# The last two blocks' down projection: two levels of seven products over both blocks at once, in place of one level for each block

## The chip, the cores and the metric

The kernel runs on one core of one Trainium2 chip. The metric is the device time of one execution in microseconds. Before the change it is 1012.9 us, the median of three runs (1011.5 to 1014.69).

A core has five engines, each with its own instruction queue, which it works through in order: TensorE (PE; its weight loads are listed as PEld), VectorE (DVE), ScalarE (ACT), GpSimd (POOL) and SyncE (SP, which issues most of the DMAs). They meet through semaphores. TensorE writes to PSUM, in banks; the others evict from there to SBUF.

## The reference

Linear attention without softmax, a root-mean-square normalisation per head, and then a feed-forward block with a gate (SwiGLU), all in fp32:

```python
def _attn_ref(q, k, v, g_norm):          # q, k, v: (8, 8, 576, 64)
    kv = np.einsum('bhsd,bhse->bhde', k, v)
    out = np.einsum('bhsd,bhde->bhse', q, kv)
    rms = np.sqrt(np.mean(out * out, axis=-1, keepdims=True) + 1e-06)
    return (out / rms * g_norm).astype(np.float32)

def _moe_ref(x, w_gate, w_val, w_out):   # x: (4608, 512), d_ff = 1536
    g = x @ w_gate
    silu = g * (1.0 / (1.0 + np.exp(-g)))
    val = x @ w_val
    return (silu * val @ w_out).astype(np.float32)
```

## The kernel before

**Tiling.** The 4608 tokens are cut into nine blocks of 512. Blocks 0 to 2 go alone, then blocks (3, 4), (5, 6) and (7, 8) go as pairs. Each block or pair has an up phase (x by w_gate and w_val, then h = silu(g) * v) and a down phase (h by w_out); the attention of later blocks is placed into the gaps. All large products use Winograd's form of Strassen's scheme: a 2x2 block product with seven products in place of eight, with sums of the operands before and sums of the results after. The seven are numbered 1 to 7. `CHAIN` tells which PSUM tile each adds into: 1, 6, 7, 4 build up in one "b" bank one after another, 2 in "a", 5 and 3 in "c". Between two products of a chain the running value is read out, so TensorE may not start product 6 before product 1's value has been evicted, and so on.

**The up phase of a pair** (`Pair.up`, `Inner`, matmuls at L816) uses two levels, 7 x 7 = 49 products for each pair j of 128-wide columns of h, and there are six j. The outer products are taken in four groups g of up to two; in each group the seven inner products follow, one 128x256 matmul for each outer product. `Inner.sequence` weaves the last two products of a group into the next group. The 49 weights of a j were written to DRAM earlier and are read back through 14 DMAs (`Stream`, L906) into a pool of nine tiles `t`; `Stream.pump`, called after each product, issues the next load when the tile nine places back has been given up. All of them go through SP's queue.

VectorE evicts each product, adding it onto an earlier group's result. Four times in a j, GpSimd adds group 1's finished quarter (U2) to the result of outer product 5 (P5) into a third room, from where VectorE's evictions of group 3 read it (`made1`). Then GpSimd makes one more sum (`made2`), the two products silu(g) * v for both blocks (`made3`, 128x1024 each), and block a's two sums of h (`h_sums`). For the last j VectorE does the last two. Results live in a ring of five rooms `r`.

**The down phase** (`Ffn.down`, `Down`, matmuls at L661) uses one level, for block a and then for block b: seven products, each six steps times two halves, 84 matmuls of 128x256 for a block. Their stationary operand is h and their moving operand w_out; the result is in row order. The sums on w_out for products 5, 7 and 4 are made by GpSimd into tiles of the same pool (`turn_t`). For the last two blocks `down.lone` is set: nothing is left to weave in, so product 3 goes into an own bank "m" (`third`, L1032) and is placed earlier, and the last block (`final`) keeps its halves in banks apart, so that the last output half can be stored early (`store`, L1122).

**What sets the order.** Each engine's order is fixed when the program is built: by the order in which the code records instructions, by `tc.issue_after` (an instruction may not stand ahead of a given one), and by `in_order`, which pins an engine to the recorded order. Before, the pair's down phases pin TensorE.

The small sums and products all record through helpers, so their lines are L130 (add), L131 (subtract) and L132 (multiply) wherever they are used.

Of the kernel before, what the change touches and what calls it, by code (L numbers as in the profile page):

```python
# [14 lines left out]
P = 128  # L15
# [3 lines left out]
def kernel(  # L19
# [114 lines left out]
    @contextmanager  # L134
    def in_order(*engines):

        traced = nc.cur_bb.bb.instructions
        last = traced[-1]
        yield
        start = next(k for k in reversed(range(len(traced))) if traced[k] is last) + 1  # L140
        before = {}
        for i in traced[start:]:
            if engines and i.engine not in engines:
                continue
            if i.engine in before:
                tc.add_manual_dep(
                    i, before[i.engine].name,
                    mybir.DependencyInfo(mybir.DependencyClass.NoSync, mybir.DependencyReason.DATA), reason="order",
                )
            before[i.engine] = i  # L150

# [488 lines left out]
    class Quad:  # L640


        def __init__(self, steps):
            self.steps = steps
            self.ps, self.room = {}, None

            self.apart = {}

# [3 lines left out]
        def multiply(self, p):  # L652
            name, first = CHAIN[p]
            if first:
                tiles = [PSUMS[name].tile([P, 2, HB], F32, name=name) for _ in range(1 + (name in self.apart))]
                self.ps[name], self.apart[name] = tiles[0], tiles[-1]
            banks = self.ps[name], self.apart[name]
            for e, i in self.order(p):
                lhsT, rhs = self.operands(p, e, i)

                self.ffn.multiplied = nc.tensor.matmul(  # L661
                    banks[e][:, e], lhsT=lhsT, rhs=rhs, start=first and i == 0 and (e == 0 or banks[0] is not banks[1]),
                    stop=i == self.steps - 1, skip_group_check=True,
                )
            getattr(self, f"after{p}", lambda: None)()
# [91 lines left out]
    class Inner:  # L757
# [94 lines left out]
        def made3(self, p, e, q):  # L852
            if p != 4:
                return
            h = h_both[:, :, 2 * self.j : 2 * self.j + 2]
            halves = lambda t: t.rearrange("p (b e) t -> p b e t", b=2)
            c11, c12, c21, c22 = (self.whole(*i) for i in ((1, 1), (3, 1), (3, 0), (1, 0)))

            engine = nc.gpsimd if self.j + 1 < NP else nc.vector
            mul(engine, h[:, :, :, 0:HB], halves(c11), halves(c12))  # L860
            with tc.issue_after(self.ffn.fifth.ins):
                nc.scalar.activation(out=c21, in_=c21, func=ACT.Silu)
            mul(engine, h[:, :, :, HB:BLK], halves(c21), halves(c22))
            self.ffn.ended = self.ffn.a.h_sums(self.j, 1, engine)

# [13 lines left out]
    class Stream:  # L879
# [15 lines left out]
        def pump(self):  # L895

            while self.next and not self.held[-9]:
                n, j, c = key = self.next.pop(0)
                tile_ = t_tile(key)
                os, ps = JOINT[c]  # L900
                count = len(os) * len(ps)
                self.tiles[key] = tile_.rearrange("p a (b c) -> p (a b) c", c=P)
                self.uses[key] = count
                to = self.tiles[key][:, 0:count].rearrange("p (o i) c -> p o (i c)", o=len(os))
                src = self.dram[:, j, steps_of(OUTERS, os), steps_of(INNERS, ps)].rearrange("p o i c -> p o (i c)")
                nc.sync.dma_start(out=to, in_=src)  # L906

        def use(self, n, j, o, p):
            c, i = self.joint[o, p]
            key = n, j, c  # L910
            self.uses[key] -= 1
            if not self.uses[key]:
                self.free(key)
            return self.tiles[key][:, i]
# [4 lines left out]
    stream = Stream()  # L919
# [65 lines left out]
    class Down(Quad):  # L985
        def __init__(self, ffn):
            super().__init__(NP)
            self.ffn = ffn
            self.t = {}
            self.final = ffn.n == NB - 1  # L990
            self.lone = False
            self.opens = None
            self.keeps = False
            if self.final:
                self.apart["c"] = None
# [16 lines left out]
        def multiply(self, p, es=(0, 1)):  # L1012
            if p == 3 and self.lone:
                self.third(es)
                return
# [7 lines left out]
        def third(self, es):  # L1023


            if es[0] == 0:
                tiles = [m_psum.tile([P, 2, HB], F32, name="m") for _ in range(1 + self.final)]
                self.thirds = tiles[0], tiles[-1]
            for e in es:
                for i in range(self.steps):  # L1030
                    lhsT, rhs = self.operands(3, e, i)
                    self.ffn.multiplied = nc.tensor.matmul(  # L1032
                        self.thirds[e][:, e], lhsT=lhsT, rhs=rhs, start=i == 0 and (e == 0 or self.final),
                        stop=i == self.steps - 1, skip_group_check=True,
                    )
            if not self.final:
                add(nc.vector, self.o1[:, :, HD:DM], self.thirds[0], self.u2)
                self.ffn.store(self.o1, 0)
                return
            for e in es:  # L1040
                add(nc.vector, self.o1[:, e, HD:DM], self.thirds[e][:, e], self.u2[:, e])
                self.ffn.store(self.o1[:, e : e + 1, HD:DM], e, slice(HD, DM))

        def after6(self):
            super().after6()
            if self.lone:
                self.add_c(self.u2, self.u2)

        def order(self, p):
            order = [(e, i) for e in range(2) for i in range(self.steps)]  # L1050
            return order if p == 3 and self.final else sorted(order, key=lambda ei: ei[1])
# [17 lines left out]
        def rows(self):  # L1069
            o = ring()  # L1070
            self.o1, self.o2 = o[:, 0:2], o[:, 2:4]

        def after2(self):
            if self.lone:
                self.rows()
            add(nc.vector, self.o1[:, :, 0:HD], self.ps["a"], self.s)
            if self.final:
                self.ffn.store(self.o1[:, :, 0:HD], 0, slice(0, HD))
# [4 lines left out]
        def after7(self):  # L1083
            if not self.lone:
                self.rows()
            u3 = self.piece(2)
            nc.scalar.copy(out=u3, in_=self.ps["b"])
            self.add_c(self.o2[:, :, HD:DM], u3)
# [5 lines left out]
        def after3(self):  # L1094
            self.add_c(self.o1[:, :, HD:DM], self.u2)
            if not self.final:
                self.ffn.store(self.o1, 0)
                return
            for e in range(2):
                self.ffn.store(self.o1[:, e : e + 1, HD:DM], e, slice(HD, DM))  # L1100

        def add_c(self, o, u):

            if not self.final:
                add(nc.vector, o, self.ps["c"], u)
                return
            for e, c in enumerate((self.ps["c"], self.apart["c"])):
                add(nc.vector, o[:, e], c[:, e], u[:, e])

    class Ffn:  # L1110
# [9 lines left out]
        def store(self, o, t, columns=slice(None)):  # L1120
            rows = out[BLK * self.n : BLK * (self.n + 1), columns].rearrange("(t p) d -> p t d", t=T)
# [40 lines left out]
        def down(self, nxt, then={}):  # L1162
# [3 lines left out]
            down.lone = nxt is None  # L1166
            order = (1, 6, 5, 7, 2, 4, 3) if 5 in fill else (1, 5, 6, 7, 2, 4, 3)
            if down.lone:
                order = (1, 5, 6, 2, 7, 3, 4)
            for p in order:  # L1170
# [5 lines left out]
                with tc.issue_after(nxt.multiplied.ins) if self.n == 0 and p in (5, 6) else ExitStack():  # L1176
                    down.multiply(p, *[(0,)] * (p == 3 and down.lone and down.final))
# [14 lines left out]
            if down.lone and down.final:  # L1192
                down.multiply(3, (1,))
# [25 lines left out]
    class Pair:  # L1219


        def __init__(self, n):
            self.n = n
            self.a, self.b = (Ffn(i, blocks[i]) for i in (n, n + 1))
            self.visited = None

        def up(self, fill):

            a = self.a
            a.s1 = s_pool.tile([P, NP, HB], F32, name="s1")  # L1230
# [5 lines left out]
            for i, this in enumerate(units):  # L1236
                for unit, p in this.sequence(last):
                    if unit:
                        visited, self.visited = self.visited, None
                        with tc.issue_after(visited.ins) if visited else ExitStack():  # L1240
                            unit.multiply(p)
                last = this
                fill.get(i + 1, lambda: None)()
            a.down_ = Down(a)
            a.down_.keeps = True
            a.down_.turn_t(5)
# [3 lines left out]
            a.ended = self.ended  # L1250
# [165 lines left out]
    for n in range(PAIRED, NB, 2):  # L1416
# [3 lines left out]
        if after:  # L1420
# [10 lines left out]
            for i in range(8):  # L1431
                fill[12 + i] = lambda i=i, after=after: after[i // 4].load_quarters(i % 4 // 2, (i % 2,))
        pair.up(fill)
        if after:
            after[0].turn()
        if len(after) > 2:
            after[2].load_kv(0)
        with in_order(nc.tensor.engine):
            pair.a.down(after[0] if after else None, {5: pair.second_sums})
            if after:  # L1440
                after[1].turn()
            if len(after) > 2:
                after[2].load_kv(1)
            pair.b.down(after[1] if after else None)
# [31 lines left out]
```

## Time and profile before

| | us |
|---|---|
| median of the runs | 1012.9 |
| the profiled execution | 1012.7 |
| its span, first to last instruction | 1010.9 |
| TensorE busy | 993.7 |
| VectorE busy | 673.7 |
| GpSimd busy | 369.6 |
| ScalarE busy | 232.2 |

The granted TensorE clock is full in this execution. A fp32 matmul of the large products is recorded as two passes, so 84 matmuls show as 168. "Busy" of TensorE is not TensorE at its peak, since matmuls are pipelined. Times in timelines are microseconds from the start of the span. In a group's row the last part is the idle time of the engine just before these instructions, and which instruction ended it.

### The profile page before, as it was taken

The numbers are of one execution on the slowest core, as the hardware profiler recorded it, in microseconds if no ns is written. First come the engines' busy times: TensorE is split into PE (matmuls) and PEld (weight loads), VectorE is DVE, ScalarE is ACT, GpSimd is POOL, SyncE is SP. The second block draws the span as 40 slices with busy tenths as digits, with TensorE's granted clock in tenths as the row PEclk, the third lists the DMA queues.
The fourth block names the chain that finished last, engine by engine and source line by source line (L and its number), as shares of the span: only waits on it lengthen the run. The fifth ranks groups of instructions, "written<-read, shape, count | busy, mean of one in ns | idle before, by whom it ended". The sixth has DMA issues, their size and how long they took to land.

```text
span 1010.9 us, 17078 instructions
## 1 busy us (share of the span) xinstructions
PE 993.7 (98%) x6506; PEld 831.6 (82%) x6506; DVE 673.7 (67%) x1121; ACT 232.2 (23%) x367; POOL 369.6 (37%) x290
## 2 busy tenths in 40 slices
PE   5999999999999999999999999999999999999998
PEld 4544688888888888888888888888888888888887
DVE  2999797589868477656676746666668566666311
ACT  2665111221122311212211121121112121121000
POOL 0000263255544240445456004455660026546600
PEclk9999999999999999999999999999999999999999
DMA  8688653483866855767742464667221654553011
GB/s 220 198 266 260 120 93 136 97 288 97 210 136 122 214 114 158 189 179 182 170 130 42 111 164 135 182 164 191 77 42 43 146 164 144 150 145 101 1 42 42
DMA packets 254290, 143.23 MB, mean 142 GB/s; under 512 B 149504, under 2 KB 236544, under 8 KB 254208
## 3 DMA queue, kind: packets, MB, share of 16 engines
q1 hardware_dynamic: 223488, 138.20, 50.8%
q10 hardware_dynamic: 30656, 3.94, 2.5%
q8 instruction: 52, 0.85, 0.4%
q14 instruction: 30, 0.25, 0.1%
q0 software_dynamic: 64, 0.00, 0.0%
HBM read 104.99 MB, written 28.70 MB: 132 GB/s over the span
## 4 chain that ended last, share of the span: by engine, by line
PE 75%; DMA 1%; POOL 0%; SPq 0%; issue 0%; DVE 0%; POOLq 0%
PE b L816 22%; PE b L661 20%; PE c L816 11%; PE c L661 9%; PE a L816 5%; PE a L661 5%; PE m L431 1%; PE m L1032 1%; PE m L370 1%; DMA ld<-in_v_dram 1%; POOL t L131 0%; SPq L312 0%; PE b L370 0%; PE b L431 0%; PE a L431 0%
## 5 line engine op out<-in xcount | busy, mean ns | idle before, releaser
L816 PE MATMUL b<-arena,t 128*128 128x256 f32 x1008 | 244.5, 381 | 0.0
L816 PEld LDWEIGHTS b<-arena,t 128*128 128x128 f32 x1008 | 190.1, 190 | 29.6 <-DVE r L130 2.4
L130 POOL TENSOR_TENSOR r<-r 128x256 f32<-128x256 f32 (+1 forms) x90 | 94.7, 1054 | 246.1 <-DVE r L130 154.9
L130 DVE TENSOR_TENSOR r<-b,r 128x512 f32<-128x512 f32 (+1 forms) x234 | 138.9, 606 | 60.1 <-PE b L816 54.8
L130 DVE TENSOR_TENSOR r<-c,r 128x512 f32<-128x512 f32 (+1 forms) x170 | 104.5, 623 | 81.9 <-PE c L816 40.1
L132 POOL TENSOR_TENSOR arena<-r 128x1024 f32<-128x1024 f32 (+1 forms) x54 | 102.1, 1904 | 112.3 <-DVE r L130 67.9
L131 POOL TENSOR_TENSOR t<-wo 128x512 f32<-128x512 f32 x54 | 76.9, 1445 | 167.8 <-DVE wo L130 105.9
L130 DVE TENSOR_TENSOR r<-a,r 128x512 f32<-128x512 f32 x93 | 59.2, 636 | 108.3 <-PE a L661 70.7
L816 PE MATMUL c<-arena,t 128*128 128x256 f32 x504 | 122.5, 379 | 0.0
L131 DVE TENSOR_TENSOR arena<-arena 128x512 f32<-128x512 f32 (+3 forms) x96 | 104.3, 1101 | 20.0 <-PE b L661 17.7
L816 PEld LDWEIGHTS c<-arena,t 128*128 128x128 f32 x504 | 95.6, 190 | 13.5 <-issue 0.3
L661 PE MATMUL b<-wo,arena 128*128 128x256 f32 x432 | 98.1, 382 | 0.2
L661 PE MATMUL b<-t,arena 128*128 128x256 f32 x432 | 96.2, 379 | 0.0
L661 PEld LDWEIGHTS b<-wo,arena 128*128 128x128 f32 x432 | 81.2, 190 | 12.5 <-DVE arena L132 0.9
L661 PEld LDWEIGHTS b<-t,arena 128*128 128x128 f32 x432 | 82.1, 190 | 11.2
L830 ACT COPY r<-b 128x512 f32<-128x512 f32 x54 | 31.7, 586 | 189.9 <-PE b L816 189.9
L131 POOL TENSOR_TENSOR t<-arena 128x512 f32<-128x512 f32 x36 | 51.1, 1432 | 56.2 <-PE c L661 21.9
L816 PE MATMUL a<-arena,t 128*128 128x256 f32 x252 | 66.1, 379 | 0.0
L816 PEld LDWEIGHTS a<-arena,t 128*128 128x128 f32 x252 | 47.9, 190 | 6.5
L661 PE MATMUL c<-t,s 128*128 128x256 f32 x216 | 48.1, 379 | 0.0
L661 PE MATMUL a<-wo,arena 128*128 128x256 f32 x216 | 48.1, 379 | 0.0
L661 PEld LDWEIGHTS a<-wo,arena 128*128 128x128 f32 x216 | 41.0, 190 | 5.6
(115 smaller groups left out, 1242.9 us busy)
## 6 DMA issues: line engine op xcount, KB each, us to landing
t<-w SPq DMA_DIRECT2D x180, 256.0 KB, 3.1
out_dram<-r SPq DMA_DIRECT2D x17, 512.0 KB, 2.9
ld<-in_k_dram SPq DMA_DIRECT2D x26, 288.0 KB, 4.6
ld<-in_v_dram SPq DMA_DIRECT2D x26, 288.0 KB, 6.1
t<-w SPq DMA_DIRECT2D x54, 128.0 KB, 2.3
ld<-in_moe_w_gate_dram SPq DMA_DIRECT2D x12, 512.0 KB, 4.6
ld<-in_moe_w_val_dram SPq DMA_DIRECT2D x12, 512.0 KB, 4.7
ld<-in_moe_w_out_dram SPq DMA_DIRECT2D x12, 512.0 KB, 4.8
```

The lines of the kernel that those rows point to most:

```text
L130: add = lambda e, o, a, b: e.tensor_tensor(out=o, in0=a, in1=b, op=OP.add)
L131: sub = lambda e, o, a, b: e.tensor_tensor(out=o, in0=a, in1=b, op=OP.subtract)
L132: mul = lambda e, o, a, b: e.tensor_tensor(out=o, in0=a, in1=b, op=OP.mult)
L370: self.positions = nc.tensor.matmul(self.kv_ps[r][u * D : (u + 1) * D, g, :], lhsT=k[:, u, c, :], rhs=v[:, u, c, :], start=(c == 0), stop= ...
L431: self.multiplied = nc.tensor.matmul(self.ps[i][u][p : p + D, t, j, :], lhsT=self.qt[rows, tile_t, head, p : p + D], rhs=kvs[b % 3][rows, ...
L661: self.ffn.multiplied = nc.tensor.matmul(banks[e][:, e], lhsT=lhsT, rhs=rhs, start=first and i == 0 and (e == 0 or banks[0] is not banks[1 ...
L816: self.ffn.multiplied = nc.tensor.matmul(ps[:, i], lhsT=stream.use(self.ffn.n, self.j, o, p), rhs=self.operand(o, p), start=first and i == ...
L830: copied = nc.scalar.copy(out=dst, in_=ps)
L1032: self.ffn.multiplied = nc.tensor.matmul(self.thirds[e][:, e], lhsT=lhsT, rhs=rhs, start=i == 0 and (e == 0 or self.final), stop=i == self ...
```

## The change

The last pair (blocks 7 and 8) gets its own down phase, `Deep.down`, with both blocks together and two levels: 7 outer times 7 inner products, each of three steps c over d_ff, so 147 matmuls of 128x256. Now w_out is the stationary operand and h of both blocks the moving one, so the result is transposed: it is turned back at the end, two quadrants by VectorE's transposes of 32x32 pieces with the rest done in 32 small stores (`send`, half on ACT's queue, half on SP's), two by 16 TensorE transposes (`turn_back`).

The sums on w_out move to GpSimd in the pair's up phase (`Deep.prepare`, given out by `tick` after each product at the places in `TURNS`, every place in the first fourteen): six sums in place on w_out; nine blocks of differences for outer products 5, 7 and 4, each written to DRAM from the one buffer `temp` and read back later as 21 leaf tiles; and twelve differences for outer products 1, 2, 6 and 3, kept in SBUF. GpSimd also makes the h sums for both blocks, at least twelve places after h (`made`), and the inner sums of h for two of the three steps (`turn`). The remaining sums of h (`sum_x`, `outer`) are VectorE's, between the products of the down phase, whose order is written out by hand and pinned for TensorE and VectorE. The `lone` and `final` branches of the old down phase are removed; no other block used them.

```diff
+        def turned_block(self, i, c):
+            temp, rows = self.temp[:, 0:7], slice(2 * c, 2 * c + 2)
+            raw = temp[:, 0:4].rearrange("p (k n) d -> p k (n d)", k=2)
+            b, t2o = (self.quadrant(o)[:, rows] for o in ((3, 1, 2)[i], 6))
+            def differences():
+                sub(nc.gpsimd, temp[:, 4], temp[:, 0], temp[:, 1])
+                sub(nc.gpsimd, temp[:, 5:7], temp[:, 2:4], temp[:, 1:2].to_broadcast([P, 2, P]))
+                nc.sync.dma_start(out=self.dram[:, i, c], in_=temp)
+            return [lambda: sub(nc.gpsimd, raw, b, t2o), differences]
...
+            for i in range(3):
+                for c in range(3):
+                    self.later += self.turned_block(i, c) + [kept.pop(0)]
+            self.later += kept
+
+        TURNS = {0: (0, 1), 1: (), 2: (4, 5, 6), 3: (0, 2, 4, 5)}
+
+        def tick(self):
+            g, e = divmod(self.count % 28, 7)
+            self.count += 1
+            if e not in self.TURNS[g] and self.count > 14:
+                return
+            steps = self.due if self.due and self.due[0][0] <= self.count else self.later
+            step = steps.pop(0) if steps else None
+            if step:
+                with behind(nc.gpsimd.engine):
+                    (step[1] if steps is self.due else step)()
...
+        def sum_x(self, x, *os):
+            for o in os:
+                a11, a12, s2, a22 = (self.part(o, k, q) for k, q in ((0, 0), (1, 0), (0, 1), (1, 1)))
+                to = self.extras[o][:, x]
+                if x == 0:
+                    add(nc.vector, to, s2, a11)
...
+        def down(self):
...
+            m(2, 7)
...
+            add(nc.vector, v, u2, c22)
+            self.sum_x(0, 3)
+            m(2, 3)
+            self.sum_x(1, 3)
+            m(3, 1)
+            self.sum_x(2, 3)
+            room = ring().rearrange("p (o a) x -> p o (a x)", o=2)
+            add(nc.vector, c11, p1, c11)
+            m(2, 4)
+            nc.vector.transpose(out=room[:, 0], in_=c11)
+            self.send(room[:, 0], 0, 0, nc.scalar)
+            m(3, 6)
+            add(nc.vector, c22, u3, c22)
+            m(3, 5)
+            nc.vector.transpose(out=room[:, 1], in_=c22)
+            self.send(room[:, 1], 1, 1, nc.sync)
+            m(3, 2)
+            m(3, 7)
+            self.rows = ring().rearrange("p (e q) (o f d) -> p e q o f d", e=2, o=2, f=2)
+            m(3, 3)
+            self.turn_back(0, 0)
+            self.turn_back(1, 1)
+            m(3, 4)
+            self.turn_back(1, 0)
+            self.turn_back(0, 1, True)
...
+        if pair.deep:
+            stream.leaves(pair.deep)
+            pair.up(fill)
+            with in_order(nc.tensor.engine, nc.vector.engine):
+                pair.deep.down()
+            continue
```

## The prediction

> **What bounds the kernel now.** I read the page's busy times and slices, the chain that ended last, the groups with shapes kept apart, then the timelines of GpSimd and VectorE in the last pair, and the DMA issues.
>
> ```profile
> PE 993.7 (98%) x6506; PEld 831.6 (82%) x6506; DVE 673.7 (67%) x1121; ACT 232.2 (23%) x367; POOL 369.6 (37%) x290
> POOL 0000263255544240445456004455660026546600
> ```
>
> TensorE has work for 98% of the span; GpSimd has none in the last two slices and about half of each slice ahead of them. By stretch (busy us of TensorE, its weight loads, VectorE, ScalarE, GpSimd), the last pair's up and down phases:
>
> ```profile
> 807.80:935.00 127.20, 127.20 (x589) 111.45 (x588) 84.95 (x144) 25.71 (x35) 65.79 (x53) 1.00 0.47 140
> 935.00:1008.00 73.00, 72.54 (x337) 63.52 (x335) 16.77 (x20) 5.75 (x9) 16.29 (x12) 1.00 0.08 28
> ```
>
> GpSimd has 61 us to spare in the first, VectorE 56 us in the second.
>
> ```profile
> 910.22 0.86 PE a L816 x4
> ...
> 933.97 1.05 PE b L816 x4
> 935.02 5.18 PE b L661 x24
> ...
> 1004.95 2.60 PE m L1032 x12
> 1007.55 0.02 issue
> 1007.58 0.42 DVE r L130
> ```
>
> The chain is TensorE without a gap: the up phase of 127.2 us, then the two down phases to 1007.5. A 128x256 product is recorded as two passes; 24 passes take 5.18 us, so a pass takes 0.216 and a product 0.432 us. Fewer products are worth that much each, if nothing else comes late.
>
> ```profile
> L132 POOL TENSOR_TENSOR arena<-r 128x1024 f32<-128x1024 f32 x30 | 70.2, 2361 | 60.7 <-DVE r L130 60.7
> L130 POOL TENSOR_TENSOR r<-r 128x256 f32<-128x256 f32 x72 | 52.3, 728 | 187.8 <-DVE r L130 96.6 <-DMA t<-w 89.1
> L132 DVE TENSOR_TENSOR arena<-r 128x1024 f32<-128x1024 f32 x6 | 7.1, 1222 | 0.3
> 818.28 1.53 POOL L130 TENSOR_TENSOR r<-r 128x256 f32<-128x256 f32 x2 [59.84 <-DVE r L130]
> 820.81 0.72 POOL L130 TENSOR_TENSOR r<-r 128x256 f32<-128x256 f32 x1 [1.00 <-DVE r L130]
> 832.59 4.68 POOL L132 TENSOR_TENSOR arena<-r 128x1024 f32<-128x1024 f32 x2 [3.79 <-DVE r L130]
> 923.46 1.28 POOL L131 TENSOR_TENSOR t<-wo 128x512 f32<-128x512 f32 x1
> 844.27 0.69 DVE L130 TENSOR_TENSOR r<-b,r 128x512 f32<-128x512 f32 x1 [0.36 <-PE b L816]
> t<-w SPq DMA_DIRECT2D x180, 256.0 KB, 3.1
> w<-arena SPq DMA_DIRECT2D x10, 384.0 KB, 3.5
> out_dram<-r SPq DMA_DIRECT2D x17, 512.0 KB, 2.9
> ```
>
> In the up phase GpSimd's U2 + P5 pieces (818.28 to 822.9) are read by VectorE's evictions of group 3, so GpSimd can hold up VectorE, and VectorE holds a bank that TensorE wants.
>
> [...] the up phase's evictions read one from PSUM, and GpSimd's 128x1024 products stay at 2.34 each there, so I take uncontended durations. [...] the rows above show 2.9 to 3.5 us for writes of 384 and 512 KB.
>
> **The change: TensorE.** Removed: 2 x 84 = 168 products of L661 and L1032. Added: 49 x 3 = 147 of the same shape, and 16 transposes of 128x128 (L494: 16 in 2.3 us, 0.14 each). 21 x 0.432 = 9.1 us saved; 8 transposes stand ahead of the last product (1.2 us).
>
> **The change: VectorE in the down phase.** It had 16.8 us to do there. Now: 33 sums of 128x768, not in the trace; 0.69 us at 512 and 1.22 at 1024 bound them, and I take 0.95: 31.4 us. Evictions: 13 x 0.69 + 11 x 0.42 = 13.6. Five operations at 1024, 1.22 each: 6.1. Two transposes at 1.22: 2.4. Six sums of 512 at 0.70: 4.2. Two copies: 0.8. Together 58.5 us, under TensorE's 147 x 0.432 + 16 x 0.14 = 65.8, but in a fixed order. Walking that order from the start of down: VectorE is 3 us ahead at the first extras, level with TensorE when the sums for outer product 5 are made (18 to 27 us), and about 3 us behind around 45 us, where V, the sums for 4 and 3 and the first eviction of group 3 are queued. There inner product 6 of group 3 waits for that eviction about 1.5 us (none with sums at 0.87, 2.5 with 1.0). Then TensorE leads again. **The end:** last product at 66.4, its eviction 0.2 + 0.7, four transposes 0.6 + 0.2, two copies 0.8: VectorE ends at 68.8 us, where before it took 73.0 from the start of down (935.0 to 1008.0). The 32 small stores of 32 KB go out from 53 us (ACT) and 57 us (SP). Issues of 64 KB pieces took 0.63 us, so sixteen take 10 us and leave SP free at about 67.5, just in time for the last four tiles; up to 1 us more if slower. The store after it is 128 KB as before. **Down gives 4.2 us (2.5 to 5.5).**
>
> **The change: GpSimd in the last up phase.** Kept: 24 pieces at 0.73, six sums and ten products at 2.36: 55.3 us. Added: six sums on w_out at 1.28 (7.7); nine leaf blocks, each 512 + 128 + 256 wide, 1.28 + 0.45 + 0.73 (22; the 0.45 is the line through 256 and 512); twelve 384-wide differences at 1.0 (12); ten h sums at 1.28 (12.8, replacing 7.3); eight turned sums at 1.28 (10.2). 120 us of 127 where it had 65.8: it fits over the whole phase, but most comes first, in the engine's fixed order. There is one buffer for a leaf block: each block's first subtraction waits until the last block's 448 KB write to DRAM has landed. That write is not in the trace; 2.9 to 3.5 us bound it, I take 3.2.
>
> Walk down GpSimd's queue as the changed program orders it, from the up phase's start (0 = 807.8); "wanted" is when VectorE or TensorE came to that point before (its evictions at 823.1, 824.0, 825.3 and 844.27). The w_out sums may start as the last product of the block before frees w_out, at -4, and end at 4.5 (with 0.08 between dependent operations). Block 1 ends at 7.1, its write lands at 10.4. A 1.0 us difference covers part of that. Block 2 starts at 10.5 and ends at 13.1, landing at 16.4. Piece 1 runs to 14.9: VectorE wants it at 15.4. Block 3 starts at 16.5; piece 2 stands inside it, done at 18.6, wanted at 16.2; piece 3 at 20.5, wanted at 17.5. The eviction behind it frees TensorE's bank at 21.3, not 18.6: **2.7 us lost.** Block 4 ends at 26.0, U2's sum at 29.4, block 5 at 32, block 6 at 38, the two products for h at 42.8 (29.5 before), the next unit's first piece at 43.6. It was wanted at 36.5.
>
> **Past SP's queue.** The nine writes sit among the weight loads on SP, which issues in order. Write 4 stands ahead of the tile that the 57th product reads at 24.6 us; that load was free to go at 16. It goes at 26.5 and lands at 30.3 (3.0, and 0.8 behind the write): TensorE, by then due at 27.3, waits **3 us**. The late piece takes **1** more (43.6 against 36.5 + 5.7 + 0.4 of slack). Write 7 goes at 52.1, and the load behind it lands at 56.3, wanted at 46.7 + 6.7: **3**. Writes 8 and 9 cost about **0.6 and 1.** After j = 2 GpSimd has caught up, since the delay has also moved its deadlines. Sum 11.3; rounding down, since the waits share slack, **10 us (4 to 14)**: writes that land in 2.6 us take about 3 off, loads that land in 4.5 add 3. ScalarE is 23% busy and hides its copies; the h sums that now follow U2 + P5 cost nothing in themselves, since nothing reads them before down.
>
> **Sum.** The profiled execution took 1012.7 (span 1010.9), 0.2 from the median of 1012.9. 1012.7 + 10 - 4.2 = 1018.5 us.
>
> **Rivals.** A, *the up phase covers it* (faster): the down gain of 4.2 stands and GpSimd and SP stay hidden: 1008.5. For it: GpSimd idles 60 us before this phase, and 120 fits into 127. Against: even with no wait for a write (5 us less by block 4), block 4 ends at 21, where its load must leave at about 21.2; it decides when the writes land in under 2 us, below every write of this size in the trace. B, *half hidden* (same): only the late pieces cost, the loads behind the writes have more slack than I see: 5 us lost, 1013.5. For it: the phase moved 150 GB/s without a wait. C, *both phases stall*: 768-wide sums at 1.05 and SP's small stores put down at no gain, the up phase loses 12: 1025. For it: VectorE at 58.5 of 66 in a fixed order; against: the next-nearest row, 896 wide with two SBUF inputs, took 1.0 to 1.1.
>
> **How the numbers follow.** Forecast 1018.5, 0.60, its own range 1014 to 1024; A 0.15; B 0.14; C 0.11. The range reaches from A's time to C's, 1008 to 1025. What a measurement of this kernel can tell from no change is about 0.3%, 3 us. Faster is A and no more: 0.15. Same is B and a sliver of the forecast: 0.16. Slower: 0.69.
>
> **What would show it.** TensorE's new products at 0.216 a pass; GpSimd busy about 407 us in all; the up phase ending near 945 in place of 935, its gaps in the first half, released by VectorE's evictions and by weight loads; down about 69 us long. I am wrong if the first three units of the up phase still take 21.2 us each, if the leaf writes land in 2 us, or if down takes over 72.

## The result and the profile after

| | before | after |
|---|---|---|
| median of 5 runs, us | 1012.67 | 1019.59 |
| lowest to highest | 1011.43 to 1014.69 | 1016.83 to 1023.13 |
| ratio, with its 95% interval | | 1.0069 (1.0040 to 1.0097) |
| up phase of the last pair, profiled, by the starts in the chain | 127.3 | 140.6 |
| down phase to VectorE's end, profiled | 73.0 | 66.7 |

The changed kernel is slower by 6.9 us, where 5.8 were forecast. Its profiled execution took 1023.1 us, near the top of the runs: it comes to the last up phase at 810.5 us, where other runs of the same code up to there come at 806 to 809. So I compare lengths of phases, not ends.

The page's first two parts, TensorE's and the other engines' busy times and GpSimd's slices:

```profile
PE 991.2 (97%) x6480; PEld 826.1 (81%) x6480; DVE 717.0 (70%) x1174; ACT 233.1 (23%) x370; POOL 408.8 (40%) x328
POOL 0000364255544241445565004554660478877100
```

GpSimd has 39 us more to do (forecast 407 in all) and its busiest slices are where it had idled. The last up phase by busy times, columns as in the prediction's table of stretches (the last three are the granted clock, the busy share of the DMA engines and GB/s):

```profile
810.53:951.16 140.63, 129.91 (x589) 110.44 (x589) 87.62 (x146) 25.69 (x35) 115.58 (x101) 1.00 0.54 166
```

TensorE stands still for 10.7 of 140.6 us; before, it was busy for all of the 127.20 in the prediction's row. The other 2.7 us are its busy time, 129.9 for the same products: a group that starts after a gap is recorded longer (1.53 us for six passes, 1.29 from start to start otherwise; a single pass is recorded as 0.38 us, while in a row one starts every 0.216, so the records overlap). Where it stands, from TensorE's timeline (start, length, instruction, and in brackets the idle time before it and what ended it):

```profile
828.87 1.56 PE L817 MATMUL b<-arena,t 128*128 128x256 f32 x6 [1.78 <-DVE r L130]
834.02 1.99 PE L817 MATMUL b<-arena,t 128*128 128x256 f32 x8 [2.72 <-DVE r L130]
841.81 1.97 PE L817 MATMUL b<-arena,t 128*128 128x256 f32 x8 [1.30 <-DMA t<-w]
...
867.21 1.13 PE L817 MATMUL b<-arena,t 128*128 128x256 f32 x4 [1.94 <-DMA t<-w]
875.44 1.53 PE L817 MATMUL c<-arena,t 128*128 128x256 f32 x6 [1.16 <-DMA t<-w]
```

First it waits for VectorE's evictions, which wait for GpSimd's pieces; from 840 us on mostly for weight loads. (None of GpSimd's 290 instructions before and 328 after works on a bank of PSUM; in both traces VectorE and ScalarE alone evict.) GpSimd's timeline over the first of these:

```profile
808.15 1.99 POOL L130 TENSOR_TENSOR wo<-wo 128x512 f32<-128x512 f32 x1
814.26 1.27 POOL L131 TENSOR_TENSOR wo<-wo 128x512 f32<-128x512 f32 x1
823.97 1.27 POOL L131 TENSOR_TENSOR s<-wo 128x512 f32<-128x512 f32 x1 [3.69 <-DMA leaf<-s]
827.37 0.73 POOL L130 TENSOR_TENSOR r<-r 128x256 f32<-128x256 f32 x1
829.52 1.26 POOL L131 TENSOR_TENSOR s<-wo 128x512 f32<-128x512 f32 x1 [1.43 <-DMA leaf<-s]
```

The second leaf block waits 3.7 us for the first one's write, and the first piece for U2 + P5 (827.37) is queued behind that block. SP's own timeline says what became of the loads:

```profile
843.79 0.33 SPq L945 DMA_DIRECT2D leaf<-s  x1
844.22 2.12 SPq L1220 DMA_DIRECT2D t<-w  x4
849.84 0.32 SPq L945 DMA_DIRECT2D leaf<-s  x1
```

Four loads leave in 2 us as soon as the write at 843.79 has left, then the queue stands again until the next write can go at 849.84: loads move in bursts behind the writes. The end of down, from the chain that ended last:

```profile
1012.11 0.87 PE m L1085 x8
1012.98 2.61 PE b L893 x12
```

TensorE runs without a gap to 1015.6, 64.4 us from the start of down (951.16). VectorE's last two copies end at 1017.88, 66.7 us from it. The expectations below have 66.4, which is the end of the first of the two.

### The profile page after: what moved, and what is told of

Its sections match the earlier page's. It is cut to its first block, busy times and chain, and to the rows that moved or that the text cites. A ratio compares the mean times of both kernels' runs of the same rounds, so it can differ in the third digit from the quotient of the medians.

```text
span 1021.2 us, 17221 instructions
## 1 busy us (share of the span) xinstructions
PE 991.2 (97%) x6480; PEld 826.1 (81%) x6480; DVE 717.0 (70%) x1174; ACT 233.1 (23%) x370; POOL 408.8 (40%) x328
## 4 chain that ended last, share of the span: by engine, by line
PE 71%; DMA 3%; POOL 1%; DVE 1%; SPq 0%; issue 0%; ACT 0%; DVEq 0%; POOLq 0%
PE b L817 20%; PE b L662 15%; PE c L817 10%; PE c L662 8%; PE a L817 5%; PE a L662 4%; PE b L893 4%; PE c L893 2%; DMA t<-w 2%; PE m L435 1%; PE a L893 1%; PE m L374 1%; POOL s L131 1%; DMA ld<-in_v_dram 1%; DMA leaf<-s 1%; POOL r L130 0%
## 5 line engine op out<-in xcount | busy, mean ns | idle before, releaser
L817 PE MATMUL b<-arena,t 128*128 128x256 f32 x1008 | 245.3, 381 | 9.2 <-DVE r L130 5.3
L130 DVE TENSOR_TENSOR r<-b,r 128x512 f32<-128x512 f32 (+1 forms) x247 | 146.1, 603 | 76.2 <-PE b L817 59.8
L131 POOL TENSOR_TENSOR t<-wo 128x512 f32<-128x512 f32 x45 | 65.6, 1480 | 163.8 <-DVE wo L130 107.9
L131 DVE TENSOR_TENSOR arena<-arena 128x512 f32<-128x512 f32 (+4 forms) x117 | 122.9, 1068 | 9.2 <-PE b L662 6.9
L662 PE MATMUL b<-wo,arena 128*128 128x256 f32 x336 | 77.8, 386 | 0.2
L662 PE MATMUL b<-t,arena 128*128 128x256 f32 x336 | 74.8, 379 | 0.0
L662 PEld LDWEIGHTS b<-wo,arena 128*128 128x128 f32 x336 | 63.7, 192 | 10.3 <-DVE arena L132 0.9
L662 PEld LDWEIGHTS b<-t,arena 128*128 128x128 f32 x336 | 63.8, 190 | 8.7
L662 PE MATMUL b<-arena 128*128 128x256 f32 x192 | 45.5, 380 | 0.0
L662 PE MATMUL b<-arena,t 128*128 128x256 f32 x192 | 45.4, 379 | 0.0
L1469 PE MATMUL b<-arena 128*128 128x512 f32 (+1 forms) x104 | 43.5, 561 | 0.5 <-ACT arena L499 0.5
```

The source lines that it names most:

```text
L130: add = lambda e, o, a, b: e.tensor_tensor(out=o, in0=a, in1=b, op=OP.add)
L131: sub = lambda e, o, a, b: e.tensor_tensor(out=o, in0=a, in1=b, op=OP.subtract)
L662: self.ffn.multiplied = nc.tensor.matmul(ps[:, e], lhsT=lhsT, rhs=rhs, start=first and i == 0 and e == 0, stop=i == self.steps - 1, skip_g ...
L817: self.ffn.multiplied = nc.tensor.matmul(ps[:, i], lhsT=stream.use(self.ffn.n, self.j, o, p), rhs=self.operand(o, p), start=first and i == ...
L1469: nc.tensor.matmul(t, lhsT=w[f // 2][:, i, P * (f % 2) : P * (f % 2 + 1)], rhs=x[:, i, of], start=(i == 0), stop=(i == NS - 1),)
```

## The experiments

The reading to test, called T below: the up phase loses 13 us because GpSimd's w_out steps come late, by waits for the one buffer, and SP's queue, which issued in order at the writes of 843.79 and 849.84 above, holds weight loads behind the late leaf writes. Rivals: the traffic of the writes (D), GpSimd's amount of work (R), the burst of steps at the start (O'). "Up" is the last pair's up phase in the profiled execution, by the starts in the chain. "At half clock" is how long TensorE was granted 0.50 of its clock within it; the change itself had none of that there.

| run | what differs from the change | up, us | of it at half clock | median, us | ratio to before (95%) |
|---|---|---|---|---|---|
| e1 | no w_out sums, writes or leaf loads | 127.3 | 0 | 1006.43 | 0.9940 (0.9922 to 0.9957) |
| e5 | leaf loads, no w_out sums; the nine writes leave far ahead of the phase | 127.3 | 0 | 1006.70 | 0.9945 (0.9928 to 0.9961) |
| e2 | two buffers | 134.6 | 3.4 | 1014.30 | 1.0025 (1.0015 to 1.0034) |
| e6 | steps spread from tick 7 | 135.4 | 6.8 | 1015.11 | 1.0021 (1.0012 to 1.0030) |
| e3 | writes on GpSimd's queue | 141.6 | 6.8 | 1020.42 | 1.0082 (1.0067 to 1.0097) |
| e8 | e3 and e6 | 141.5 | 13.6 | 1017.79 | 1.0054 (1.0035 to 1.0074) |
| e4 | e2 and e3 | 134.1 | 3.4 | 1013.76 | 1.0015 (1.0007 to 1.0022) |
| e9 | all w_out sums on VectorE | 134.5 | 0 | 1014.04 | 1.0016 (1.0009 to 1.0022) |
| e10 | twelve of them on VectorE | 137.7 | 3.4 | 1017.40 | 1.0048 (1.0033 to 1.0063) |
| e11 | e2 and e6 | 132.2 | 0 | 1011.15 | 0.9988 (0.9977 to 0.9998) |
| e12 | e11, writes later in SP's queue | 127.3 | 0 | 1006.65 | 0.9947 (0.9932 to 0.9962) |
| e13 | e2, writes later in SP's queue | 127.3 | 0 | 1006.72 | 0.9947 (0.9927 to 0.9967) |

**e1 and e5: where the loss is.** e1 lets down read w_out as it lies; e5 adds to that the nine writes (from w_out, without sums) and the leaf loads.

```diff
         def prepare(self):
...
+            return
             for c in range(3):
...
-            stream.leaves(pair.deep)
```

```diff
+            self.later += [
+                lambda i=i, c=c: nc.sync.dma_start(out=self.dram[:, i, c], in_=...)
+                for i in range(3) for c in range(3)
+            ]
+            return
```

> Leaves out all sums on w_out in the last up phase, the nine leaf writes and the 21 leaf loads; the new down phase reads w_out as it lies, with the same 147 matmuls, VectorE sums and stores. Theory (the up phase loses its time only because GpSimd is made late by the w_out sums and SP's weight loads queue behind the leaf writes): the up phase is back at 127.2 us, down stays at 66.4, and the time is 1012.7 - 6.6 + 0.8 = about 1007. Rival (the h sums for both blocks on GpSimd, or the new down phase, carry a part of the loss): the up phase stays above 129 us and the time above 1009.

> Leaves out all GpSimd sums on w_out, but keeps nine 448 KB writes to DRAM on SP's queue, one place of the first nine after another, from w_out as it lies, and the 21 leaf loads. Theory (a write costs nothing when nobody on GpSimd is late): up phase 127 to 128.5 us, time about 1007 to 1008. Rival (the writes' traffic itself delays the weight loads and so TensorE): up phase 131 us or more, time 1011 or more.

Both up phases are as long as before, and down is as in the change. So the w_out steps cost 13 us (1019.6 - 1006.4), all of it in the up phase. But e5 does not test rival D: its writes had nothing to wait for, and they left SP long before the phase, as its trace shows (the last two times are the first and last start):

```profile
L958 SPq DMA_DIRECT2D leaf<-wo x9: 326/831/1273, 124.7 to 152.0; - x9
```

Its expectation came true without the test; only the leaf loads stood where they stand in the change. What decides about D are the runs below that issue the same writes inside the phase and have no product waiting for a load: e3, e8 and e4, and above all e12 and e13, which have no gap at all.

**e2 and e6: two ways to make GpSimd less late.** In e2 odd blocks use another tile, the rest of `temp` and a free `kvs` tile, with two DMAs for their write.

```diff
-            temp, rows = self.temp[:, 0:7], slice(2 * c, 2 * c + 2)
+            odd, rows = (3 * i + c) % 2, slice(2 * c, 2 * c + 2)
+            temp = self.temp[:, 7:12] if odd else self.temp[:, 0:7]
+            tail = kvs[0].rearrange("p (a b) d -> p a (b d)", a=2) if odd else temp[:, 5:7]
```

> The leaf blocks alternate between two buffers, so a block no longer waits for the write just ahead of it. Theory: the 8.4 us that GpSimd waited for the four writes go; block 4 ends near 22 us of the up phase in place of 28, its load lands about 1.5 us late, the second unit's first piece comes in time; the up phase loses 1 to 5 us (130 us long) and the time is about 1009. Rival (GpSimd has simply too much work in the phase, with or without the wait): the up phase still loses 8 us or more, 1014 or more. Rival (the leaf writes slow the weight loads down): the same.

```diff
-            if e not in self.TURNS[g] and self.count > 14:
+            if e not in self.TURNS[g] and self.count > 7:
```

> The stretch in which every place is given a GpSimd step ends after 7 places in place of 14, so the same work is spread over the phase. Theory (the loss is from too much at the start, not from the whole): the first unit's pieces come in time, the writes stand later among the weight loads; the up phase loses 3 to 6 us in place of 13, time about 1010 to 1012. Rival (the whole of the work is too much): the loss moves to later units and stays at 10 us or more, 1016 or more.

Each wins back 5 to 6 us of the up phase, less than expected; e2 still loses 7.3 us, which lies nearer to its rivals' 8 than to T's 1 to 5. With two buffers no product waits for a late piece any more; what is left in both are waits for weight loads behind a leaf write. In e6 one of them, 3.5 us long, has an aftermath that the table of stretches shows:

```profile
884.00:886.96 2.96, 2.90 (x7) 2.40 (x8) 0.69 (x1) 0.00 (x0) 1.43 (x3) 0.50 1.02 328
886.96:889.50 2.54, 2.54 (x7) 2.00 (x7) 0.85 (x2) 0.00 (x0) 0.68 (x1) 0.50 0.46 153
```

TensorE is granted half its clock from 883.2 to 890.0 us, the last 5.9 us of it after the stall, and three groups of 1.29 us take 7.05 us together: a stall of 3.5 us cost 3.2 us more. A shorter gap can be followed by the same. In e4:

```profile
830.02 3.60 PE L817 MATMUL b<-arena,t 128*128 128x256 f32 x8 [2.17 <-DVE r L130]
830.24:833.65 3.41, 3.41 (x9) 2.70 (x9) 1.34 (x3) 0.00 (x0) 3.33 (x5) 0.50 0.06 25
```

A gap of 2.2 us was followed by 3.4 us at half clock, and so was one of 2.6 us in e2, while a gap of 2.7 us in the change left the clock at 1.00. So the length of a gap alone doesn't decide, and no run shows what does. In e2 the two groups of six passes behind that gap take 4.35 us from start to start (843.04 to 847.39), where two such groups behind a gap of the change take 2.66 (848.71 to 851.37): about 1.7 us of what e2 still loses is this aftermath.

**e3, e8 and e4: the writes leave SP's queue.**

```diff
-                nc.sync.dma_start(out=self.dram[:, i, c], in_=temp)
+                nc.gpsimd.dma_start(out=self.dram[:, i, c], in_=temp)
```

> The nine leaf writes are issued from GpSimd's own queue instead of SP's; the sums, their order and their one buffer stay. Theory T (SP's queue issues in order, so that a leaf write that waits for late GpSimd sums holds up the weight loads behind it): the waits of products for w's loads late in the up phase go (about 12 us of them in the chain of the changed kernel), the late pieces from GpSimd of the first 20 to 40 us of the phase stay, and each issue costs GpSimd itself something; the up phase of the last pair takes 133 to 137 us instead of 140.6 and the time is 1011 to 1015. Rival theory D (the weights are late because the leaf traffic occupies the DMA engines or the memory): the waits for w's loads stay whichever queue issues the writes, time 1018 or more.

> Leaf writes on GpSimd's queue, and w_out's steps on GpSimd one tick in two or so already from tick 7 instead of tick 14; one buffer as in the change. Theory T: the early steps no longer make the first unit's pieces late (the spread alone had no stall before 880 us), and what the spread alone still lost, 3.4 and 4.1 us of waits for weight loads behind a leaf write in SP's queue, goes with the queue; up phase 127 to 129 us, time 1006 to 1009, below the kernel before. Rival (GpSimd has too little room in this phase whatever the order, 120 us of work in 127): the waits come back as waits for GpSimd's pieces, up phase 131 or more, time 1011 to 1015.

> Two buffers for the leaf blocks and the writes on GpSimd's queue; w_out's steps at the same early ticks as in the change. Theory T: no wait of GpSimd for a write, no weight load behind a write; what stays is the start of the phase, where nine steps of w_out run ahead of the first unit's pieces beside VectorE's sums: 5 to 8 us, up phase 132 to 135 us, time 1010 to 1013. If the early burst of steps itself costs nothing, time 1006 to 1008.

The expectations of e3 and e8 missed; e4's up phase fell into its range, and its time came out 0.8 us above. In each, waits for loads are gone from TensorE's timeline, as T had it and D did not. But in e3 and e8 more waits for late pieces have come in their place (in e3 3.3, 2.9 and 2.6 us for the first three), and TensorE runs at half clock after some of them. GpSimd's timeline in e3:

```profile
815.04 0.60 POOL L945 DMA_DIRECT2D leaf<-s  x1 [0.30 <-POOL s L131]
820.01 1.27 POOL L131 TENSOR_TENSOR s<-wo 128x512 f32<-128x512 f32 x1 [3.33 <-DMA leaf<-s]
```

An issue takes GpSimd 0.3 us of waiting for its own last sum and 0.56 to 0.60 us of work; the wait for the landing stays. Nine of these are 8 us, which an engine with 120 of 127 us to do doesn't have. The move did free SP, and that was worth 0.5 us with two buffers (134.1 against e2's 134.6, each with 3.4 us at half clock) and nothing with one, where the issue stood in a queue that was as full; there the clock took its part of it.

**e9 and e10: the sums leave GpSimd.** e9 puts all of w_out's sums on VectorE, one at every fourth product; e10 only the twelve of 384.

```diff
-                sub(nc.gpsimd, temp[:, 4], temp[:, 0], temp[:, 1])
+                sub(nc.vector, temp[:, 4], temp[:, 0], temp[:, 1])
...
+            if self.count % 4 == 1 and self.later:
+                with behind(nc.vector.engine):
+                    self.later.pop(0)()
```

> All of w_out's sums of this phase run on VectorE, one at every fourth product from the first, instead of on GpSimd; the one buffer and the writes on SP's queue stay, and so do h's steps on GpSimd at their ticks. Theory R (room: GpSimd has some 120 us of work and 8 us of waits for writes in 127 us, so its pieces come late wherever the w_out steps are put): GpSimd falls to about 76 us, VectorE rises from 88 to about 110 of 127, no piece and no leaf write is late, up phase 127 to 129 us, time 1006.5 to 1009, below the kernel before. Rival O (order: 33 steps more in the queue of an in-order engine whose results TensorE waits for, and leaf writes ahead of weight loads): the stall moves to VectorE's sums and the SP queue still stands, up phase 132 or more, time 1012 or more.

> Only the twelve 384-wide differences that stay in SBUF (1.0 us each on GpSimd) move to VectorE, at the same ticks; all else is the change. Two of the twelve lie in the burst of the first 14 ticks. Theory R: GpSimd's work falls from 120 to 108 us and the up phase of the last pair from 140.6 to 129 to 133 us, time 1008 to 1012. Theory O' (only the burst at the start makes GpSimd late, and the rest follows from it): the burst is 2 us shorter, up phase 137 to 139 us, time 1016 or more.

e9 came out as rival O had it for VectorE, which had 119.8 us to do where about 110 was expected (no product waited for a load), with a price that I hadn't foreseen. VectorE's timeline, then GpSimd's, of e9:

```profile
826.33 2.24 DVE L131 TENSOR_TENSOR s<-wo 128x512 f32<-128x512 f32 x1
835.77 2.25 DVE L131 TENSOR_TENSOR s<-wo 128x512 f32<-128x512 f32 x1
```

```profile
825.67 2.35 POOL L130 TENSOR_TENSOR r<-r 128x1024 f32<-128x1024 f32 x1 [2.58 <-DVE r L130]
832.61 4.86 POOL L132 TENSOR_TENSOR arena<-r 128x1024 f32<-128x1024 f32 x2 [4.59 <-DVE r L130]
```

A sum that takes VectorE 0.68 us alone takes 2.2 us where GpSimd has an operation under way, and ends 0.55 us after it (828.6 and 838.0 against GpSimd's 828.0 and 837.5). The nine of them average 1.68 us. TensorE then waits for the evictions queued behind. e10 makes R fall in its simple form: GpSimd has 106.6 us to do, 9 less than in the change, and the up phase is only 2.9 us shorter; its waits for the buffer grew from 8.4 to 11.1 us. The number that e10 gave is the one I had put down for O', but e13 below takes away that reading of it too.

**e11, e12 and e13: the place of a write in SP's queue.** e11 has two buffers and the spread. In e12 each write also enters SP's queue 12 products after its block's differences, behind the loads that are queued by then, or ahead of the next block that needs the buffer; e13 is e12 with the change's own ticks.

```diff
+                self.writes.append((self.count + 12, odd, write))
...
+        def write_out(self, odd=None):
+            for w in list(self.writes):
+                if w[0] <= self.count or w[1] == odd:
+                    self.writes.remove(w)
+                    with behind(nc.sync.engine):
+                        w[2]()
```

> Two buffers for the leaf blocks and the spread of the steps from tick 7, writes on SP's queue: no wait for a write and no burst, with all 120 us still on GpSimd. Theory R: the waits of 8 us go, but 120 of 127 us leaves GpSimd late by a few us somewhere, and a leaf write behind it holds up SP's weight loads: up phase 130 to 134 us, time 1009 to 1013. Theory O' (burst and single buffer are the whole cause): up phase 127 to 128 us, time 1006 to 1008.

> Two buffers and the spread of the steps from tick 7 as before, and each leaf write enters SP's queue 12 products later than its block's differences, behind the weight loads queued by then (four to eight loads later at the blocks that held SP up). Nothing of the work changes. Theory Q (what is left of the loss with two buffers and the spread, 4.3 and 4.4 us of waits for weight loads and slow matmuls after them, is only SP's queue standing at a write whose block GpSimd has not finished): no wait of a product for w's loads over 0.5 us, up phase 127 to 128.5 us, time 1006 to 1008, below the kernel before. Theory R (GpSimd has no room): with the loads on time the products wait for GpSimd's pieces instead, up phase 131 or more, time 1010 or more.

> As the run before with two buffers and late writes, but the w_out steps at the change's own ticks (one at each of the first 14). Theory Q (only SP's queue behind unfinished blocks costs time): 1006 to 1008 again, up phase 127 to 128.5 us. If the burst of steps at the start has a price of its own, through pieces that GpSimd makes late for the first two units: 1009 to 1012, with products that wait for VectorE's sums behind GpSimd's pieces before 850 us.

SP's timeline around the same write, first in e11 and then in e12:

```profile
857.02 13.06 SPq L1226 DMA_DIRECT2D t<-w  x14
880.24 0.33 SPq L951 DMA_DIRECT2D leaf<-s  x1
880.68 11.55 SPq L1226 DMA_DIRECT2D t<-w  x11
```

```profile
861.73 18.06 SPq L1242 DMA_DIRECT2D t<-w  x14
879.91 0.39 SPq L955 DMA_DIRECT2D leaf<-s  x1
882.88 12.03 SPq L1242 DMA_DIRECT2D t<-w  x10
```

In e11 SP has sent its loads by 870.1 and stands for ten microseconds at a write whose block GpSimd finishes at 880.2; eleven loads leave in a burst behind it. There are two such places, and TensorE's gaps at them come to 3.7 us of the 5.0 that e11's up phase is longer than before's. So e11 hit the number of theory R. But of R's two parts it is the write that holds up the loads which TensorE's gaps show, and e12 removes that without giving GpSimd more room. In e12 loads leave until 879.8, the write finds its block finished, and the next load only waits for a free slot. The stretches of e12, up and down:

```profile
807.00:934.40 127.40, 127.40 (x590) 111.66 (x589) 87.71 (x146) 25.69 (x35) 115.50 (x101) 1.00 0.60 183
934.40:1000.80 66.40, 65.48 (x311) 57.20 (x309) 54.78 (x73) 6.55 (x12) 0.00 (x0) 1.00 0.27 66
```

TensorE has no gap in the up phase, with GpSimd's work unchanged at 115.5 us. e13 gives the same without the spread, so with late writes the burst has no price of its own. Rival D falls here too: in e12 the nine writes leave between 825 and 902 us, the phase moves 183 GB/s against 140 before, and no product waits. Step by step: one buffer to two, 140.6 to 134.6; SP's order, 134.6 to 127.3. That is the whole loss, about half to each in this order of steps, with some 1.7 us of the second for the half clock after one wait of e2. e12 and e13 are 0.5% below the kernel before and 1.3% below the change (1006.7 against 1019.6), and stand within 0.3 us of e1, which does no w_out work at all.

## Why the prediction was right, step by step

- **The total** was 1018.5 against 1019.6, by errors that in part cancel, and that it came this close is in part luck: the up phase lost 3.4 us more than the 10 put down, and down gave 2.1 more than 4.2.
- **TensorE's share of down** was right: products at 0.432 and no others. The eight transposes ahead of the last product took 0.87 us, where 1.2 was put down.
- **VectorE in down.** The durations were right: the 768-wide sums took 0.95 as estimated, and the records taken singly add up to the 58.5 of the prediction. The step that failed is "inner product 6 of group 3 waits for that eviction about 1.5 us": no product waited, in any run. The walk took 0.95 for every sum, but in a row of them each begins about 0.08 us before the one ahead of it ends:

```profile
957.18 3.56 DVE L131 TENSOR_TENSOR arena<-arena 128x768 f32<-128x768 f32 x4
```

Four sums take 3.56 us, 0.87 for each further one, and at 0.87 the prediction itself had no wait. VectorE was busy for about 55 us of down, and close to late: from 989 to 1003 us it had one break of 0.26. So the last product ended at 64.4 us and not 66.4 (1.5 of that is the wait, 0.3 the transposes), the tail took 2.3 where 2.5 was put down, and down took 66.7 and not 68.8. Its gain of 6.3 lies outside the 2.5 to 5.5 that I gave.
- **The end.** The small stores were in time, but from VectorE's end to the end of the span it took 3.3 us, 2.9 before: 0.4 that the sum didn't have.
- **GpSimd's total** was right (408.8 against 407), and so was the verdict that it fits but comes late. **Uncontended durations** was wrong at one place: the first four w_out sums took 1.78 to 2.11 us, not 1.28, beside VectorE's sums with two SBUF inputs (three of those, 896 wide, took 6.31 us there from 806.86 on, and 3.33 before). I judged by GpSimd's products beside the up phase's evictions, 2.34 us each, and left out the sums still under way at the phase's start. It put everything after them 1.8 us later.
- **The write's landing** was 2.9 us at the median of the nine (2.8 to 4.5) where 3.2 was taken. But the first one held the next block off for 4.6 us from its issue, so block 2 began 13.4 us into the phase, not 10.5.
- **Late pieces:** one gap of 2.7 us was put down for the first unit; there were two, of 1.8 and 2.7. The 1 us for the second unit's piece isn't in the trace. **Loads behind writes** were put at 3, 3, 0.6 and 1; the waits were 1.3 and 0.6 us at 841.8 and 848.7, 1.9 and 1.2 at 867.2 and 875.4, and 0.2 later. That is 5.2 against 7.6: the order was right, the waits were smaller. One more gap, of 0.8 at 896.3, is put down by the profile to a VectorE eviction with no late piece ahead of it, and its cause stays open. The step that failed by size is the sum of waits as the whole price: the groups recorded longer after a gap, 2.7 us in all, were not in it, and 11.3 was rounded down to 10.
- **Rivals.** What A described came about in e12 and e13 and not in this kernel, and in another way than was thought. The prediction let it depend on how fast the writes land; the runs show that it depends on a second buffer and on where the write stands in SP's queue. Its remark that "even with no wait for a write" the load is just late is what e2 shows: 7.3 us still lost. C's stall in down is out in every run. B is out: the loads cost TensorE gaps of 5.2 us, more than the pieces with 4.5.

What isn't settled: whether the queue order alone, with one buffer, would win its half. A write can't be put later there than the next block's first difference, so it wasn't tried. What decides whether a gap of 2 to 3 us halves the clock is open too.

## What to carry to other kernels

A store that waits for a slow engine must not stand in an in-order issue queue ahead of loads that are already free to go: put it behind the loads that the fast engine needs before the store's data can be ready, and give its source a second buffer so that it may stand there. Adding up an engine's work (120 of 127 us here) tells whether it fits, not whether it is on time; walk the queues for that, those of the DMA issues too. Before moving work or issues to another engine to relieve one, look at what that engine shares with it and how full its own queue is: here none of the five runs that did so won back half of the loss. And read the granted clock of each phase before comparing two runs: four of these five had 3.4 to 13.6 us at half clock that the change didn't have.

## What the runs showed of the hardware that was not expected

- A VectorE sum of 512 with both inputs in SBUF stretched from 0.68 to 2.2 us beside a GpSimd operation (e9), and GpSimd's from 1.28 to 2.1 us beside such sums of 896 (the change), which themselves took 2.1 us each there and 1.1 before: each engine was slower beside the other.
- A stall of 3.5 us on TensorE (e6) was followed by 5.9 us at a granted clock of 0.50. Gaps of 2.2 (e4) and 2.6 us (e2) were followed by 3.4 us of it, while one of 2.7 us (the change) left it at 1.00.
- Records of VectorE sums that follow one another overlap by about 0.08 us: four of 0.95 us took 3.56.
- A 448 KB write issued by GpSimd took it 0.56 to 0.60 us, after 0.3 us of waiting for its own last sum; on SP the same issue took 0.33 us.
